# Seven-tap convolution and SwiGLU on one core: how the first pair of blocks is convolved and laid out

## The chip, the core and the metric

One core of a Trainium2 chip. Its engines run their own queues of instructions side by side: TensorE (PE, with a row of its own for weight loads, PEld), VectorE (DVE), ScalarE (ACT), GpSimd (POOL) and SyncE (SP), which issues most transfers (DMA). The metric is the device time of one execution in microseconds. Three timed runs of the kernel before have a median of 776.05 us (775.36 to 777.06).

## What is computed

The input x is 8 sequences of 4096 tokens of 192 channels, float32. Each channel is convolved along its sequence with seven causal taps, which are the softmax of one of eight rows of weights (24 channels a row). The 32768 tokens that result go through a SwiGLU block with 1536 hidden features:

```python
w = exp(weight - max(weight)); w = w / (sum(w) + 1e-9)          # 8 x 7
x = sum over k of w[head of channel, k] * x_padded[token + k]   # padded by 6 zeros in front
g = x @ w_gate; val = x @ w_val
out = (g * sigmoid(g) * val) @ w_out
```

The weights are held as float16, sums are float32.

## The kernel before

**Blocks and chunks.** A block is 512 tokens (TB), a pair is two blocks, so there are 64 blocks in 32 pairs. For each block the hidden features are taken in 12 chunks of 128. `Block.first` makes one chunk's gate and value in two PSUM banks: since 192 = 3 x 64, three steps each, a gate matmul on the upper 64 rows of the array beside a value matmul on the lower 64, 512 tokens long. `Block.gate` lets ScalarE apply SiLU and VectorE multiply by the value; the product h is float16. `Block.piece` multiplies h with w_out, in eight matmuls of 192 columns a chunk, one block behind the gates (`second` hands them out, four units per chunk; the last chunk of a block takes the block's own first four). Every 24 units ScalarE copies the sum out (`evacuate`) and SyncE stores it. Chunks are counted through the whole kernel: block 0 is chunks 0 to 11, block 1 is 12 to 23, block 2 begins at 24.

**Banks.** A gate has two banks (PLAN's gate), a value three (val); in block 0 the chunks in PLAN's `third` put the gate in the bank named `run` instead. So a gate waits for SiLU two or three chunks back, a value for the product three chunks back.

**The first pair.** Blocks 0 and 1 are convolved on TensorE. x is loaded (x_sb), cast to float16 (x16), turned by TensorE (`turn`, `turn_a`) and copied to SBUF with the padding in front (xcA, xcC, xcA1, xcC1). Channels 0 to 127 are A, the last 64 are C, held twice. `conv_a` multiplies shifted views of A with diagonal matrices of the taps, once with their high parts (dg["hi"]) and once with the low rests (dg["lo"]), `conv_c` does C with dg["C"]. The sums are folded: the first 256 tokens of 64 channels lie on partitions 0 to 63, the last 256 on 64 to 127. ScalarE copies them to foldA (two halves of A) and foldC. The gates want 64 channels on both halves of the partitions and 512 tokens in a row. In block 0 `double` does that: matmuls with `twin`, an identity twice over, and copies out (`unfold`, D0, D1, D2). In block 1 `spread_out` does it by transfers from foldA1 and foldC1 to D01b and D2b, four for each.

**Order by hand.** The program is written in the order in which each engine takes it. Block 0's C is convolved after its A has been doubled, and `doubleC` comes between the first gates of chunks 0 and 1. Block 1's A sums are made behind the first gates (`lateA("hi")`) and after chunk 1, `outA` follows at chunk 2, `lateC` at 4 and `outC` at 5.

**Later pairs.** They are loaded as squares of 32 tokens by 32 channels (`emit_load`: sqA in parts 0 and 1, sqB in parts 2 and 3, two transfers each; headA and headB where a sequence starts), turned by VectorE (`emit_turn`) and convolved by three engines in three groups a pair (`Group`; A of the first block, B, A of the second block): ScalarE makes the first product (`start_d`, into the PSUM bank run) and two more, VectorE adds taps to the first, GpSimd makes the rest, adds everything and writes xc (`join`). `swap` has SyncE copy xc with its partition halves exchanged (xs). `plan_group` puts the steps at chunks; PLAN's `opening` holds them for pair 1 as (turn, start, ScalarE's two, VectorE's, GpSimd's, join, swap). Pair 1's squares are issued at the start, as soon as the first two pieces of x have been turned; later ones at the chunks in PLAN's `load`, counted from 24 times the pair.

**Queues.** SyncE issues in program order: x, pair 1's squares, the first of pair 2's, the eight transfers of `spread_out`, further squares, the swaps and the outputs. GpSimd's queue first builds masks and casts x, issues the loads of w_gate and w_val in thirds of four chunks and of w_out, then works on the groups.

Of the kernel before, what the change touches and what calls it, by code (L numbers as in the profile page):

```python
# [17 lines left out]
    opening=(  # L18
# [3 lines left out]
    ),  # L22
    gate=2, val=3, lead=4, third=(5, 8, 11),
# [4 lines left out]
def kernel(  # L28
# [53 lines left out]
    def emit_load(q, part):  # L82
        head = q % ppb == 0
        if part == 2:
            squares[q, "A"] = headA if head else xpool.tile(
                [P, HIST + 2 * TB], fp32, tag="sqA", name="sqA"
            )
            squares[q, "B"] = headB if head else xpool.tile(
                [P, HIST + TB], fp32, tag="sqB", name="sqB"
            )  # L90
        for k in range(2):
# [3 lines left out]
            else:  # L95
# [3 lines left out]
            n = n // SQ + 1 - skip // SQ  # L99
            nc.sync.dma_start(  # L100
                out=tile_[quad * SQ : (quad + 1) * SQ, skip:].rearrange("p (n c) -> p n c", c=SQ),
# [82 lines left out]
    load_w(0, 4, 0)  # L184
    cast_c(nc.gpsimd.tensor_copy, 0, 2)
    cast_c(nc.gpsimd.tensor_copy, 2, 4)
    load_w(0, 4, 1)
# [4 lines left out]
    for b in range(2):  # L192
# [24 lines left out]
        for n, shape, dt in (  # L217
            ("xtA", [P, TB], fp32),
            ("xtC", [P, DB + TB], fp16),
            ("sumA", [P, 2, TB], fp32),  # L220
            ("idle", [P, 2, TB], fp32),
            ("xtA1", [P, DB + TB], fp16),
# [21 lines left out]
    def turn_a(subs):  # L244
        for s in subs:
            ins = nc.tensor.matmul(
                early["xtA"][:, ts(s, P)], x16[:, s, colA], ident, start=True, stop=True
            )
        return ins
# [8 lines left out]
    turned = turn_a((0, 1))  # L258

    if n_pairs > 1:  # L260
        sync_after(nc.sync.nop(), turned, "squares after x")
        for part, _ in PLAN["load"]:
            emit_load(1, part)
    turn_a((2, 3))
    warm(SUBS, SUBS)

    xcA, xcC, xcC1, xcA1 = (
        const_pool.tile([P, pad + TB], fp16, tag=n, name=n) for n in ("xcA", "xcC", "xcC1", "xcA1")
# [21 lines left out]
    diagonal(dg["lo"], lo)  # L290
    two = const_pool.tile([P, 1], fp32, tag="two", name="two")
    nc.scalar.copy(xcA[:, pad:], early["xtA"])
# [25 lines left out]
    def double(out, fold):  # L318
# [3 lines left out]
    foldA, foldA1 = (const_pool.tile([P, 2, TH], fp16, tag=n, name=n) for n in ("foldA", "foldA1"))  # L322
    foldC, foldC1 = (const_pool.tile([P, TH], fp16, tag=n, name=n) for n in ("foldC", "foldC1"))
    D0, D1, D2, D2b = (
        const_pool.tile([P, TB], fp16, tag=n, name=n) for n in ("D0", "D1", "D2", "D2b")
    )
    D01b = const_pool.tile([P, 2, TB], fp16, tag="D01b", name="D01b")

    def unfold(copy, out, pair):
        copy(out[:, :].rearrange("p (h t) -> p h t", h=2), pair[:, :, 0:TH])  # L330

    conv_a(early["sumA"], xcA, dg["hi"], True)
    spread(1)
# [3 lines left out]
    turn(early["xtA1"], colA, SUBS, hist=True)  # L337
    nc.vector.tensor_copy(wn[:, 1, :], tap_rows[1])
    nc.vector.tensor_copy(hi[:, 1, :], wn[:, 1, :])
    nc.vector.tensor_tensor(hi[DB:P, 1, :], wn[DB:P, 1, :], hi[DB:P, 1, :], op=ALU.subtract)  # L340
    diagonal(dg["C"], hi[:, 1, :])
    nc.scalar.copy(foldA, early["sumA"][:, :, 0:TH])
    early["xtC1"] = pool0.tile([P, DB + TB], fp16, tag="xtC", name="xtC")
    turn(early["xtC1"], colC, SUBS, hist=True)
    nc.vector.tensor_copy(xcA1, early["xtA1"][:, DB - pad :])
    pairs = [
        pool0.tile([P, 2, TB], fp32, tag=n, name=n) for n in ("sumA", "idle")
    ]
    double(pairs[0], foldA[:, 0, :])
    double(pairs[1], foldA[:, 1, :])  # L350
    sumC = pool0.tile([P, TB], fp32, tag="taps0", name="taps0")
    conv_c(sumC, xcC)
    unfold(nc.scalar.copy, D0, pairs[0])
    unfold(nc.vector.tensor_copy, D1, pairs[1])
    nc.vector.tensor_copy(xcC1, early["xtC1"][:, DB - pad :])
    nc.scalar.copy(foldC, sumC[:, 0:TH])
# [16 lines left out]
    class Group:  # L373
# [17 lines left out]
        def start_d(self):  # L391
            self.aD = tpool.tile([P, TB], fp32, tag="run", name="run")
# [34 lines left out]
    class Block:  # L427
# [20 lines left out]
        def first(self, j, steps=range(3)):  # L448
# [5 lines left out]
            lo, hi = self.operands()  # L454
            for i in steps:
                (a, ca), (b, cb) = lo[i], hi[i]
                nc.tensor.matmul(g, w[0:DB, ca, f], a[0:DB, :], start=(i == 0), stop=(i == 2))  # L457
                nc.tensor.matmul(v, w[DB:P, cb, f], b[DB:P, :], start=(i == 0), stop=(i == 2))  # L458
# [50 lines left out]

    def doubleC():  # L510
        for (r, _), bank in zip(sides, pairC):
            nc.tensor.matmul(bank[:, 0:TH], twin[r, :], foldC[r, :], start=True, stop=True)
        for (r, t0), bank, copy in zip(sides, pairC, (nc.scalar.copy, nc.vector.tensor_copy)):
            copy(D2[:, t0 : t0 + TH], bank[:, 0:TH])

# [3 lines left out]
    A, B = (D01b[:, 0, :], D01b[:, 1, :]), D2b  # L519
    early_operands = [((d, 0), (e, 1), (f, 2)) for d, e, f in ((D0, D1, D2), (*A, B))]  # L520
    early_operands = [(o, o) for o in early_operands]
# [39 lines left out]
    def late_sums():  # L561
        late["sum"] = apool.tile([P, 2, 512], fp32, tag="acc", name="acc")

    def lateA(part):
        if part == "hi":
            late_sums()
        conv_a(late["sum"], xcA1, dg[part], part == "hi")

    def lateC():
        late_sums()  # L570
        conv_c(late["sum"][:, 0, :], xcC1)

    def spread_out(out, fold):
        for r, _ in sides:
            for half, (f, _) in enumerate(sides):
                nc.sync.dma_start(out=out[r, ..., half * TH : (half + 1) * TH], in_=fold[f])  # L576
# [141 lines left out]
```

## Time and profile before

| | |
|---|---|
| time of the profiled execution | 773.12 us |
| its span | 771.4 us |
| median of the timed runs | 776.05 us |
| granted clock of TensorE | 1.00 |
| weight loads busy (PEld) | 599.6 us, 78% |
| instructions | 27963 |
| first gate matmul | 10.03 us |
| x_sb's four transfers | 3.1 us to landing |
| w_out's transfer | 10.1 us to landing |
| first pair that uses xs | 37.29 us |

The span is the time from the first to the last record of the trace; the rest of the reported time lies around it. In a row of stages the columns are: from and to, length, then busy time (and instructions) of PE, PEld, DVE, ACT and POOL, granted clock, share of the DMA engines' time (above one where packets overlap) and GB/s. A timeline row has its start, its length, engine, line, operation, what it writes and reads, how many were merged, and in brackets the idle time before it and what ended it. A group's row has busy time and mean nanoseconds of one, then the idle time before it. SPq rows are SyncE's issues, not the transfers themselves.

### The profile page before, as it was taken

What the parts mean: (1) busy time and instruction counts of PE and PEld (TensorE: products, weight loads), DVE (VectorE), ACT (ScalarE), POOL (GpSimd) and SP (SyncE); (2) the same over time, 40 slices, a digit from 0 to 9 for tenths busy, and PEclk for the clock granted to TensorE, in tenths of its full rate; (3) what the DMA queues carried; (4) which work ended last, traced back from release to release, by engine and by line L of the source; (5) the groups of instructions that cost most, each with busy time, mean ns of one, the idle gap of its engine ahead of it and who ended that gap; (6) DMA issues with size and microseconds to landing.
All of it is one profiled execution on the core that took longest, in us unless ns stands there. A gap on an engine that the chain in (4) does not pass through costs nothing.

```text
span 771.4 us, 27963 instructions
## 1 busy us (share of the span) xinstructions
PE 764.5 (99%) x10881; PEld 599.6 (78%) x10881; DVE 658.0 (85%) x1042; ACT 662.6 (86%) x1189; POOL 666.9 (86%) x643
## 2 busy tenths in 40 slices
PE   9899999999999999999999999999999999999998
PEld 4577777777878878888887888888888888888886
DVE  6788888888888888888888888898888888888875
ACT  7788888888888888888888888888888888888875
POOL 7798988888988889988889888899888899888850
PEclk9999999999999999999999999999999999999999
DMA  9434344433444434444334444334343434443211
GB/s 179 96 82 88 84 90 86 92 88 78 89 92 90 88 82 89 86 86 100 82 81 83 97 82 94 86 82 87 82 98 83 89 86 86 89 90 87 65 47 53
DMA packets 255670, 67.36 MB, mean 87 GB/s; under 512 B 207920, under 2 KB 255536, under 8 KB 255536
## 3 DMA queue, kind: packets, MB, share of 16 engines
q1 hardware_dynamic: 252720, 63.80, 39.6%
q0 software_dynamic: 2800, 1.77, 1.7%
q8 instruction: 85, 1.39, 0.8%
q14 instruction: 49, 0.40, 0.2%
q10 hardware_dynamic: 16, 0.00, 0.0%
HBM read 29.55 MB, written 25.17 MB: 71 GB/s over the span
## 4 chain that ended last, share of the span: by engine, by line
PE 99%; DMA 0%; SPq 0%; DVE 0%; ACT 0%; issue 0%; DVEq 0%
PE val L458 49%; PE acc L469 34%; PE gate L457 13%; PE idle L229 0%; PE acc L669 0%; DMA D2b<-foldC 0%; PE sumA L304 0%; PE acc L304 0%; SPq L576 0%; PE val L669 0%; PE run L669 0%; PE taps L312 0%; PE acc L312 0%; PE xtC L240 0%; DVE dghi L280 0%; ACT silu L462 0%
## 5 line engine op out<-in xcount | busy, mean ns | idle before, releaser
L464 DVE TENSOR_TENSOR h<-silu,val 128x512 f16<-128x512 f16 x768 | 509.0, 680 | 102.7 <-ACT silu L462 69.9
L462 ACT ACTIVATE silu<-gate 128x512 f16<-128x512 f32 x768 | 453.2, 594 | 79.5 <-PE gate L457 75.0
L469 PE MATMUL acc<-wo_sb,h 64*128 64x192 f16 x6048 | 469.0, 243 | 0.0
L415 POOL TENSOR_TENSOR t<-t,t 128x512 f32<-128x512 f32 x310 | 393.9, 1271 | 65.4 <-ACT t L386 44.8
L469 PEld LDWEIGHTS <-h 64*128 64x128 f16 x6048 | 399.3, 94 | 58.7
L458 PE MATMUL val<-xc,w_sb 64*128 64x512 f16 x1116 | 409.7, 376 | 0.0
L457 PE MATMUL gate<-xc,w_sb 64*128 64x512 f16 x1116 | 409.7, 376 | 0.0
L457 PE MATMUL gate<-xs,w_sb 64*128 64x512 f16 x1116 | 360.0, 376 | 0.0
L458 PE MATMUL val<-xs,w_sb 64*128 64x512 f16 x1116 | 360.0, 376 | 0.0
L458 PEld LDWEIGHTS <-w_sb 64*128 64x128 f16 x2304 | 208.9, 94 | 98.5 <-DMA D01b<-foldA 1.2
L457 PEld LDWEIGHTS <-w_sb 64*128 64x128 f16 x2304 | 208.7, 94 | 4.6 <-issue 1.4
L421 POOL TENSOR_TENSOR xc<-t,aD 128x512 f16<-128x512 f32 x93 | 118.2, 1271 | 7.3
L408 POOL TENSOR_SCALAR t<-xtA,wn 128x512 f32<-128x512 f32 x155 | 106.2, 697 | 2.0 <-DVE xtA L111 2.0
L386 ACT ACTIVATE t<-xtA,wn 128x512 f32<-128x512 f32 x124 | 88.4, 713 | 0.0
L507 ACT COPY o<-acc 128x384 f32<-128x384 f32 x126 | 60.4, 479 | 18.9 <-PE acc L469 8.4
L403 DVE SCALAR_TENSOR_TENSOR aD<-xtA,wn,run 128x512 f32<-128x512 f32 x62 | 46.0, 741 | 0.0
L386 ACT ACTIVATE t<-xtB,wn 128x512 f32<-128x512 f32 x62 | 44.3, 715 | 0.0
L408 POOL TENSOR_SCALAR t<-xtB,wn 128x512 f32<-128x512 f32 x62 | 42.4, 698 | 0.5 <-DVE xtB L111 0.5
L393 ACT ACTIVATE run<-xtA,wn 128x512 f32<-128x512 f32 x62 | 42.5, 686 | 0.2 <-DVE xtA L111 0.2
L111 DVE STREAM_TRANSPOSE xtA<-sqA 128x544 f32<-128x544 f32 (+1 forms) x48 | 34.6, 721 | 0.0
L403 DVE SCALAR_TENSOR_TENSOR run<-xtB,wn,run 128x512 f32<-128x512 f32 x31 | 23.2, 750 | 0.8 <-ACT run L393 0.8
L403 DVE SCALAR_TENSOR_TENSOR run<-xtA,wn,run 128x512 f32<-128x512 f32 x31 | 23.2, 750 | 0.0
(102 smaller groups left out, 172.9 us busy)
## 6 DMA issues: line engine op xcount, KB each, us to landing
out_dram<-o SPq DMA_DIRECT2D x127, 192.0 KB, 2.0
sqA<-in_x_dram SPq DMA_DIRECT2D x96, 132.0 KB, 3.1
xs<-xc SPq DMA_DIRECT2D x186, 64.0 KB, 2.0
sqB<-in_x_dram SPq DMA_DIRECT2D x96, 68.0 KB, 2.4
headA<-in_x_dram SPq DMA_DIRECT2D x28, 128.0 KB, 2.9
headB<-in_x_dram SPq DMA_DIRECT2D x14, 68.0 KB, 2.2
headB<-in_x_dram SPq DMA_DIRECT2D x14, 64.0 KB, 2.5
x_sb<-in_x_dram SPq DMA_DIRECT2D x4, 192.0 KB, 3.1
```

The lines of the kernel that those rows point to most:

```text
L386: mul(parts[-1], *self.tap(k))
L393: nc.scalar.mul(self.aD, *self.tap(0))
L403: nc.vector.scalar_tensor_tensor(out=self.aD, in0=v, scalar=s, in1=run, op0=ALU.mult, op1=ALU.add)
L408: self.product(k, lambda t, v, s: nc.gpsimd.tensor_scalar(t, v, scalar1=s, scalar2=1.0, op0=ALU.mult, op1=ALU.mult), self.parts)
L415: nc.gpsimd.tensor_tensor(self.parts[0], self.parts[0], t, op=ALU.add)
L421: nc.gpsimd.tensor_tensor(xc, self.parts[0], self.aD, op=ALU.add)
L457: nc.tensor.matmul(g, w[0:DB, ca, f], a[0:DB, :], start=(i == 0), stop=(i == 2))
L458: nc.tensor.matmul(v, w[DB:P, cb, f], b[DB:P, :], start=(i == 0), stop=(i == 2))
L462: nc.scalar.activation(s, self.g.pop(j), AF.Silu)
L464: nc.vector.tensor_tensor(h, s, self.v.pop(j), op=ALU.mult)
L469: ins = nc.tensor.matmul(acc, self.h[j][r, ts(s, P)], wo_r[r, j, :], start=first and j == 0, stop=not first and j == NCH - 1, skip_group_c ...
L507: nc.scalar.copy(self.o[:, 2 * half : 2 * half + 2, :], self.acc[:, :, 0:D])
```

## The change

Block 0's C is convolved, folded and doubled before its first gate, and `doubleC` goes. Block 1's sums of A come after chunks 1 and 3. Block 1's C is no longer convolved on TensorE: xcC1 is made in folded form, each half of the partitions with its own 256 tokens and the six before, VectorE makes taps 0 and 1, GpSimd the other five, and GpSimd's last add writes foldC1. Block 1's gates read the folded tiles themselves: each chunk in two rounds of 256 tokens, one from foldA1 and foldC1, the other from swapA1 and swapC1, whose halves are exchanged by two transfers for A and two for C. Pair 1's sqA comes in two parts, the second behind these transfers; pair 2's squares are not issued before chunk 6. Group B of pair 1 holds its running sum in SBUF (runB). Block 0's third gate bank is used from chunk 2. The first half of x is turned into two tiles; the taps of C are spread before the first sum; both loads of the first third of weights are issued before GpSimd's casts.

```diff
-        (9, 11, (12, 13), (12, 13), 12, 13, 18),
-        (None, -1, (2, 4), (-1, 2), 2, 4, 11),
-        (14, 16, (18, 20), (17,), 20, 21, 31),
+        (9, 12, (13, 14), (13, 14), 12, 14, 20),
+        (None, 1, (2, 5), (2, 4), 2, 5, 14),
+        (18, 20, (22, 23), (21,), 20, 23, 31),
     ),
-    gate=2, val=3, lead=4, third=(5, 8, 11),
+    gate=2, val=3, lead=4, third=(2, 5, 8, 11),
...
-    def emit_load(q, part):
+    def emit_load(q, part, half=None):
...
+            if half is not None:
+                first = TB // SQ + 1
+                skip, row, n = ((skip, row, first), (first * SQ, row + first * SQ, n - first))[half]
...
     load_w(0, 4, 0)
+    load_w(0, 4, 1)
...
-    turned = turn_a((0, 1))
+    turned = turn_a(0)
...
-            emit_load(1, part)
-    turn_a((2, 3))
-    warm(SUBS, SUBS)
+            emit_load(1, part, None if part > 1 else 0)
+    turn_a(2)
+    spread(1)
+    warm(SUBS)
...
     conv_a(early["sumA"], xcA, dg["hi"], True)
-    spread(1)
     turn(early["xtC"], colC, 0)
     nc.scalar.copy(xcC[:, pad:], early["xtC"][:, 0:TB])
     conv_a(early["sumA"], xcA, dg["lo"], False)
...
     nc.scalar.copy(foldA, early["sumA"][:, :, 0:TH])
+    sumC = pool0.tile([P, TB], fp32, tag="taps0", name="taps0")
+    conv_c(sumC, xcC)
+    nc.scalar.copy(foldC, sumC[:, 0:TH])
+    pairs = [pair("sumA"), pair("idle")]
     double(pairs[0], foldA[:, 0, :])
     double(pairs[1], foldA[:, 1, :])
     unfold(nc.scalar.copy, D0, pairs[0])
     unfold(nc.vector.tensor_copy, D1, pairs[1])
+    xtA1 = pool0.tile([P, DB + TB], fp16, tag="xtC", name="xtC")
+    turn(xtA1, colA, SUBS, hist=True)
+    nc.vector.tensor_copy(xcA1, xtA1[:, DB - pad :])
+    xtC1 = pool0.tile([P, DB + TB], fp16, tag="taps0", name="taps0")
+    turn(xtC1, colC, SUBS, hist=True)
+    pairs.append(pair("idle"))
+    double(pairs[2], foldC)
+    unfold(nc.scalar.copy, D2, pairs[2])
+    xcC1 = const_pool.tile([P, pad + TH], fp16, tag="xcC1", name="xcC1")
+    for r, t0 in sides:
+        nc.vector.tensor_copy(xcC1[r, :], xtC1[r, DB - pad + t0 :][:, 0 : pad + TH])
...
         def start_d(self):
-            self.aD = tpool.tile([P, TB], fp32, tag="run", name="run")
+            if (self.p, self.g) == (1, 1):
+                self.aD = const_pool.tile([P, TB], fp32, tag="runB", name="runB")
+            else:
+                self.aD = tpool.tile([P, TB], fp32, tag="run", name="run")
...
+            passes = [(g, v, *self.operands())]
+            if self.n == 1:
+                halves = [slice(0, TH), slice(TH, TB)]
+                passes = [
+                    (g[:, a], v[:, b], [(x[k], c) for *x, c in early_operands[1]],
+                     [(x[k], c) for *x, c in early_operands[1]])
+                    for k, (a, b) in enumerate((halves, halves[::-1]))
+                ]
+            for g, v, lo, hi in passes:
+                for i in steps:
+                    (a, ca), (b, cb) = lo[i], hi[i]
+                    nc.tensor.matmul(g, w[0:DB, ca, f], a[0:DB, :], start=(i == 0), stop=(i == 2))
+                    nc.tensor.matmul(v, w[DB:P, cb, f], b[DB:P, :], start=(i == 0), stop=(i == 2))
...
+    def tapC1(k):
+        return xcC1[:, k : k + TH], wn[:, 1, k : k + 1]
+    v, s = tapC1(0)
+    nc.vector.tensor_scalar(sumC1, v, scalar1=s, scalar2=None, op0=ALU.mult)
+    v, s = tapC1(1)
+    nc.vector.scalar_tensor_tensor(
+        out=sumC1, in0=v, scalar=s, in1=sumC1, op0=ALU.mult, op1=ALU.add
+    )
+    for k in range(2, K):
+        v, s = tapC1(k)
+        t = oneC1 if k > 2 else poolC1
+        nc.gpsimd.tensor_scalar(t, v, scalar1=s, scalar2=1.0, op0=ALU.mult, op1=ALU.mult)
+        if k > 2:
+            nc.gpsimd.tensor_tensor(poolC1, poolC1, oneC1, op=ALU.add)
+    nc.gpsimd.tensor_tensor(foldC1, poolC1, sumC1, op=ALU.add)
+    early_operands = [
+        (((D0, 0), (D1, 1), (D2, 2)),) * 2,
+        ((foldA1[:, 0, :], swapA1[:, 0, :], 0), (foldA1[:, 1, :], swapA1[:, 1, :], 1),
+         (foldC1, swapC1, 2)),
+    ]
...
-    def spread_out(out, fold):
-        for r, _ in sides:
-            for half, (f, _) in enumerate(sides):
-                nc.sync.dma_start(out=out[r, ..., half * TH : (half + 1) * TH], in_=fold[f])
+    def exchange(out, fold):
+        for r, q in ((0, 1), (1, 0)):
+            nc.sync.dma_start(out=out[sides[r][0]], in_=fold[sides[q][0]])
...
     def outA():
         nc.scalar.copy(foldA1, late["sum"][:, :, 0:TH])
-        spread_out(D01b, foldA1)
+        exchange(swapA1, foldA1)
     def outC():
-        nc.scalar.copy(foldC1, late["sum"][:, 0, 0:TH])
-        spread_out(D2b, foldC1)
+        exchange(swapC1, foldC1)
+        if n_pairs > 1:
+            for part in (0, 1):
+                emit_load(1, part, 1)
...
-    at_chunk(1, lambda: lateA("lo"))
-    at_chunk(2, outA)
-    at_chunk(4, lateC)
-    at_chunk(5, outC)
+    at_chunk(1, lambda: lateA("hi"))
+    at_chunk(3, lambda: lateA("lo"))
+    at_chunk(3, outA)
+    at_chunk(4, outC)
...
-            at_chunk(base + c, lambda q=q, part=part: emit_load(q, part))
+            at_chunk(max(base + c, 6), lambda q=q, part=part: emit_load(q, part))
...
                     block.first(0, (0, 1))
-                    doubleC()
                     block.first(1, (0, 1))
-                    lateA("hi")
```

86 lines of the change are left out of this document (29 added, 57 removed).

## The prediction

> **What bounds the kernel now.** I read the page's engine table first, then the busy time by stages, then the chain of waits, TensorE's and SyncE's timelines and the groups by form.
>
> ```profile
> PE 764.5 (99%) x10881; PEld 599.6 (78%) x10881; DVE 658.0 (85%) x1042; ACT 662.6 (86%) x1189; POOL 666.9 (86%) x643
> 22.00:24.00 2.00, 0.80 (x6) 0.22 (x4) 1.48 (x3) 0.92 (x2) 1.51 (x3) 1.00 0.42 82
> 24.00:28.00 4.00, 2.70 (x34) 1.69 (x33) 1.53 (x3) 2.04 (x4) 2.38 (x2) 1.00 0.48 92
> 28.00:32.00 4.00, 4.00 (x61) 2.93 (x59) 3.63 (x6) 3.47 (x7) 3.40 (x4) 1.00 0.58 115
> ```
>
> TensorE is busy 99% of the span; from 28 us to the tail every stage is full at a granted clock of 1.00. The one hole is 22 to 26 us. So a change is worth what it moves the moment from which TensorE is full, and nothing in the later stages can be won by it. TensorE's timeline and the chain say what the hole is:
>
> ```profile
> 22.36 0.39 PE L457 MATMUL gate<-D01b,w_sb 64*128 64x512 f16 x1 [0.25 <-DMA D01b<-foldA]
> 23.70 0.37 PE L458 MATMUL val<-D01b,w_sb 64*128 64x512 f16 x1 [0.95 <-DMA D01b<-foldA]
> 24.68 0.39 PE L457 MATMUL gate<-D2b,w_sb 64*128 64x512 f16 x1 [0.38 <-DMA D2b<-foldC]
> 25.98 0.39 PE L458 MATMUL val<-D2b,w_sb 64*128 64x512 f16 x1 [0.91 <-DMA D2b<-foldC]
> ...
> 24.04 1.89 DMA D2b<-foldC
> ```
>
> Block 1's first chunk waits for its unfolded operands, four times. Its six matmuls (three pairs, .215 us from pair to pair) should end .65 after they begin; the first began 22.36, the last ends its issue at 26.20. SyncE's timeline tells why the operands are late:
>
> ```profile
> 6.75 8.24 SPq L100 DMA_DIRECT2D sqA<-in_x_dram  x4
> 15.03 3.75 SPq L100 DMA_DIRECT2D sqB<-in_x_dram  x2
> 18.90 3.17 SPq L576 DMA_DIRECT2D D01b<-foldA  x4
> 22.17 2.46 SPq L576 DMA_DIRECT2D D2b<-foldC  x4
> ```
>
> foldA's copy on ScalarE (L579) ends at 15.46, but SyncE is still issuing squares until 18.8, then issues eight transfers one after another.
>
> **The change, part by part.** Every time is on the scale of this execution (span 771.4, reported time 773.12; the three timed runs have a median of 776.05, 2.93 more, which I add at the end).
>
> *Until the first gate.* Between 5.47 and 10.03 TensorE does: sumA 0.96, own taps 0.31, xtC 0.33, sumA 0.89, two transposes of block 1 at 0.46 each, two doublings 0.33 and taps 0.89. Afterwards the own taps stand before this (beside one warm-up, so nothing to gain at the start) and a third doubling, 0.22, comes in. First gate 10.0: no gain. The turn of two 128-row pieces into two tiles is worth at most 0.1, which I leave out.
>
> *Block 0.* All six pairs of its first two chunks can now run when D2's copy is done: doubling ends 10.05, copy 0.59 (L330 on ScalarE), so chunks 0 and 1 end at 11.5 (before, with one sum between, 12.55). Left until block 1: sumA twice 0.89, ten chunks at 0.645, first eight acc 0.33: 8.56, which gives 20.1. The third sum (L312, 0.89) is gone. But VectorE must follow: the product of a chunk waits for SiLU and frees the bank that the chunk three later needs. From the first product at 12.2, ten products at 0.62 from start to start and two tap steps at 0.65 (the timeline's spacing) end at 19.7 where SiLU is never late. Laying the instructions of TensorE, ScalarE and VectorE down in their queues' order with these spacings, TensorE waits 1.0 in all for products, in chunks 7, 8 and 11 (bounds nothing and 2.0; the first would give block 1 one microsecond more). Block 1 begins at 21.4, its first chunk ends at 22.05 (26.20 before). The copy of the second doubled tile and the tail are unchanged.
>
> *Operands of block 1.* Foldings stand as they are for one half of the tokens; the other half comes by two transfers instead of four (each L576 issue 0.5 to 0.8). SyncE has half the sqA packets ahead: 8.24 x 17/33 = 4.2, so it is free at 11, and pair 2's sqB no longer stands there. swapA is issued when foldA1 is copied, 15.7 at the latest, and lands (1.9 to 2.1) by 18.4. Queued behind swapC on SyncE: four half sqA, pair 2's sqB; first needed at chunk 18, some 27. wo_sb landed at 19.7 under twice the sqA packets and is wanted at 21.0. So the hole closes with 2 us to spare.
>
> *Twelve matmuls a chunk in block 1.* Pairs of 64x256 instead of 64x512. Not in the trace as such. The chain has these:
>
> ```profile
> 8.88 0.22 PE sumA L320 x2
> 9.10 0.11 PE idle L320 x2
> 9.21 0.89 PE taps L312 x14
> ```
>
> L320 is the same form (64 rows, 128 columns of weights, 256 streamed), second pair 0.11; L469, 192 streamed, goes at 0.08 a pair with a 94 ns weight load under it; L312, 7 pairs of another form, 0.127. Bounds for block 1: 12 x (6 x 0.107 - 0.645), nothing, and 12 x (6 x 0.127 - 0.645) = 1.4. I take L320: 12 x 0.015 = 0.2. The Trainium skill's TensorEngine Tiling, Feature Incompatibilities, says that column tiling switches off fast weight loading; L312 is column-tiled and the new passes are not, which would leave L312's price out, and nothing run so far tests it.
>
> By TensorE alone block 2 then begins at 21.4 + 0.98 + 10.75 (26.32 to 37.07 before, eleven chunks) + 0.2 = 33.3, against 37.07: 3.75 earlier.
>
> *GpSimd's new work.* Ten instructions of 256 elements, in front of all of pair 1's groups. GpSimd is free at 10.63 (end of wo_sb's issue). Their forms are not in the trace:
>
> ```profile
> L415 POOL TENSOR_TENSOR t<-t,t 128x512 f32<-128x512 f32 x310 | 393.9, 1271 | 65.4 <-ACT t L386 44.8 <-DVE h L464 0.7
> L408 POOL TENSOR_SCALAR t<-xtB,wn 128x512 f32<-128x512 f32 x62 | 42.4, 698 | 0.5 <-DVE xtB L111 0.5
> L179 POOL CAST x<-x_sb 128x256 f16<-128x256 f32 x2 | 0.8, 428 | 0.0
> L179 POOL CAST x<-x_sb 128x512 f16<-128x512 f32 x1 | 0.6, 619 | 0.0
> L165 POOL TENSOR_TENSOR twin<-ident 128x128 f16<-128x128 f32 x1 | 0.5, 513 | 0.1
> ```
>
> An add costs at least half of 1.271, 0.64, at most all of it; a line through 128 elements (0.513) and 512 gives 0.77; I take 0.70. A tap product lies between 0.35 and 0.70; the casts lose 30% when halved, so 0.45. Five of each 5.75, eight dependent gaps of 0.07 0.55: 6.3, bounds 5.3 and 10.4. foldC1 at 17.0, swapC lands by 19.8: in time. Then group B and group A, 2 x 0.69 + 4 x 1.33 = 6.7 each (34.60 to 39.92 is four such adds): A's join ends at 30.4. Neither waits for ScalarE's taps, which are earlier than this.
>
> *A shared way into memory.* In the change VectorE reads two operands from SBUF in three steps (sumC1's second and both of group B's, whose run was in PSUM and is now runB) and copies SBUF to SBUF in a fourth, all while GpSimd is busy. Two of VectorE's copies of as many elements, and what GpSimd did beside the second:
>
> ```profile
> 2.45 0.21 DVE L201 CAST ident<-ident 128x128 f16<-128x128 f32 x1
> 2.92 0.84 POOL L140 DMA_DIRECT2D w_sb<-in_moe_w_gate_dram  x1
> 3.42 0.57 DVE L206 COPY own<-mask 8x128 f32<-8x128 f32 x1
> ```
>
> L206 lasts until 0.23 after GpSimd's issue ends, as if it had waited. Against this, GpSimd's cast at 5.97 began under dglo's last 0.13 and took 616, the next one 619. So the cost to GpSimd lies between nothing and their length, 0.3 + 0.45 + 2 x 0.74 = 2.2; I take half, 1.1. The Trainium skill, SBUF — State Buffer, Who interferes with whom, says that a VectorE instruction with two SBUF inputs and a GpSimd one that reads SBUF exclude each other for a whole instruction; L206 agrees with it, and it would have the second rival below.
>
> *Sum.* A's join 31.5; SyncE issues two swaps (0.5 and 0.6), the last at 32.1; landing 2.0 (xs on the page) to 2.9 (this swap before, behind an output): 34.1 to 35.0, I take 34.3, as the queue is quiet there. Block 2's second pair needs it at 33.5 by TensorE and had it at 37.29. So a wait of 0.8 takes the place of one of 3.8, and the gain is 37.29 - 34.3 = 3.0. Pair 1's third group (three products, five adds: 8.7, and 3.5 to land) is there at 43.7, wanted at 46; after that GpSimd, busy 90.7 of 100 us in the later stages, gains on TensorE. 773.12 - 3.0 = 770.1; by the median 773.05.
>
> **The rivals.**
> 1. *GpSimd is in time:* adds at 0.64, no exclusion. Join 29.5, landing 32.2; TensorE's own path decides, 3.75 earlier: 772.3. If the 256-wide pairs cost 0.127 it is 2.5: 773.5. For it: GpSimd's durations vary by under 2% in the whole trace. Against: the 128-element add at 0.513.
> 2. *The exclusion costs its whole length:* join 32.6, last issue 33.2, landing 2.9: 36.1, gain 1.2: 774.85. For it: L206; against: the cast at 5.97.
> 3. *The exchange is late all the same:* transfers at 16 us still queue as sqA's did (8.7 to landing, DMA share 1.95 at 16 to 18). swapA lands at 25.0 instead of the last wait at 25.98, gain 1.0 to 1.5: 774.7. Then the change would not do what it says. Against: half the packets.
> 4. *Slower, by GpSimd:* its 256-wide instructions cost what 512-wide do. foldC1 lies 4.1 later, A's join at 35.6, swap landed 36.2 + 2.9 = 39.1 against 37.29: 1.8 slower, 777.9. It decides from where the ten instructions with their exclusions last over 10.4 (34.5 for the join). Against: the casts fall from 0.619 to 0.428 with the size.
>
> **How the numbers follow.** Forecast 0.42, rivals 0.2, 0.2, 0.1, 0.08. The forecast's own terms (1.1 either way from the exclusion, landing 0.8) give 772.2 to 774.5. The range takes in the first rival's 772.3 and the second's and third's 774.85 with half a microsecond for the spread of the runs: 772.0 to 775.3. A measurement of this kernel tells 0.2%, 1.55 us, from no change: forecast, first rival and a little of the others are faster by more, 0.70; most of rivals 2 and 3 lie within, 0.20; slower 0.10.
>
> **What would show it.** Block 1's first chunk ends near 22 with no wait for a DMA; block 1's pairs are 0.11 apart; foldC1 ends at 17 to 18; block 2's second pair waits for xs, under a microsecond, and everything later is full. Wrong it would be with a DMA wait in block 1, a product chain that holds TensorE more than 1.0 in block 0, GpSimd instructions of 256 near 0.7 and 1.27, or a second hole at block 3.

## The result and the profile after

| | before | after |
|---|---|---|
| median of the timed runs | 776.05 us (775.1 to 777.06, 5 runs) | 771.81 us (771.5 to 773.23, 5 runs) |
| time of the profiled execution | 773.12 us | 773.23 us |
| its span | 771.4 us | 771.5 us |
| first gate matmul | 10.03 us | 12.17 us |
| block 1's first gate | 22.36 us | 24.02 us |
| block 2's first gate | 37.07 us | 36.61 us |
| weight loads busy (PEld) | 599.6 us | 511.1 us |

The ratio of after to before is 0.995, with a 95% interval of 0.9936 to 0.9965: 4.2 us faster by the medians. The two profiled executions differ by 0.11 us, that is by nothing. Both statements are right, and most of this study is about how they fit together.

The stages of the changed kernel, by the table of windows (window, length, busy time and instructions of TensorE, weight loads, VectorE, ScalarE, GpSimd, then granted clock, DMA share, GB/s):

```profile
22.00:24.00 2.00, 2.00 (x25) 1.17 (x21) 1.87 (x4) 1.78 (x4) 1.92 (x2) 1.00 0.46 73
24.00:28.00 4.00, 3.60 (x74) 3.28 (x70) 3.59 (x7) 3.49 (x7) 3.84 (x5) 1.00 0.58 91
28.00:32.00 4.00, 4.00 (x86) 3.72 (x82) 3.26 (x6) 3.10 (x6) 3.76 (x4) 1.00 0.80 153
```

The hole from 22 to 26 us is gone: of the 6 us from 22 to 28 TensorE is busy for 5.60, against 3.50 before. TensorE's timeline shows block 1's first chunk without a wait for a transfer, and its pairs 0.11 us apart (columns: start, length, engine, line, operation; in brackets the idle time ahead and what ended it):

```profile
24.02 0.27 PE L483 MATMUL gate<-foldA,w_sb 64*128 64x256 f16 x1
...
24.13 0.27 PE L483 MATMUL gate<-foldA,w_sb 64*128 64x256 f16 x1
...
24.24 0.27 PE L483 MATMUL gate<-foldC,w_sb 64*128 64x256 f16 x1
...
24.35 0.27 PE L483 MATMUL gate<-swapA,w_sb 64*128 64x256 f16 x1
...
24.57 0.27 PE L483 MATMUL gate<-swapC,w_sb 64*128 64x256 f16 x1
...
27.41 0.51 PE L495 MATMUL acc<-wo_sb,h 64*128 64x192 f16 x8 [0.40 <-SPq L377]
```

The chain of waits of the same execution (start, length, what) shows where the two microseconds were lost again:

```profile
6.02 1.64 PE sumA L313 x20
8.20 1.64 PE sumA L313 x27
9.83 1.12 PE taps L321 x14
...
19.30 0.73 POOL foldC L559
20.06 0.46 SPq L612
...
26.43 0.78 SPq L103
27.41 0.51 PE acc L495 x8
```

The two sums of the opening take 1.64 us each. In the chain of before they took 0.96 and 0.89:

```profile
5.47 0.96 PE sumA L304 x28
...
7.07 0.89 PE sumA L304 x28
```

So in the changed kernel's execution TensorE runs at little more than half its speed until about 10 us; this is called half speed below, and an opening at full speed a quick one. The windows print a granted clock of 1.00 here too, but only because the trace's record of the clock begins later: at 10.28 us in this trace, at 3.79 in that of before. The slowness is read from the matmuls' lengths. And at 27.41 TensorE waits for something that no line of the diff names: L377 is a nop in SyncE's queue (`mark`), behind which the first sum of block 0's outputs stands. SyncE comes to it when swapC has waited for GpSimd's foldC (20.03) and eight issues of squares are done (27.2). TensorE waits for a mark once more, behind pair 2's swaps, which SyncE issues when GpSimd's join has ended (56.25):

```profile
57.57 0.51 PE L495 MATMUL acc<-wo_sb,h 64*128 64x192 f16 x8 [0.30 <-SPq L377]
```

### The profile page after: what moved, and what is told of

It reads as the page before. It is cut to its first block, busy times and chain, and to the rows that moved or that the text cites. A ratio compares the mean times of both kernels' runs of the same rounds, so it can differ in the third digit from the quotient of the medians.

```text
span 771.5 us, 28091 instructions
## 1 busy us (share of the span) xinstructions
PE 766.0 (99%) x10938; PEld 511.1 (66%) x10938; DVE 659.4 (85%) x1044; ACT 658.4 (85%) x1189; POOL 672.8 (87%) x653
## 4 chain that ended last, share of the span: by engine, by line
PE 96%; POOL 2%; SPq 1%; DVE 0%; issue 0%; ACT 0%; POOLq 0%; DVEq 0%
PE gate L483 59%; PE acc L495 32%; PE val L484 4%; SPq L103 1%; POOL t L432 1%; PE idle L232 0%; PE sumA L313 0%; POOL poolC L558 0%; POOL xc L438 0%; POOL oneC L556 0%; PE acc L699 0%; POOL t L425 0%; PE taps L321 0%; SPq L612 0%; PE val L699 0%
## 5 line engine op out<-in xcount | busy, mean ns | idle before, releaser
L495 PEld LDWEIGHTS <-h 64*128 64x128 f16 x6048 | 280.9, 94 | 136.2 <-SPq L377 1.5
L495 PE MATMUL acc<-wo_sb,h 64*128 64x192 f16 x6048 | 359.1, 243 | 0.7 <-SPq L377 0.7
```

The lines of the kernel that those rows point to most:

```text
L495: ins = nc.tensor.matmul(acc, self.h[j][r, ts(s, P)], wo_r[r, j, :], start=first and j == 0, stop=not first and j == NCH - 1, skip_group_c ...
```

## Experiments

All of the kernels compute the whole result. "Before" beside a ratio is the kernel before on the same chip, measured in the same session. There were three sessions after the first, one for experiments 1, 2 (its first kernel) and 3, one for 4 to 6 and the rest of 2, one for 7 and 8; the medians of before lie between 775.8 and 776.2 in all four, so a few tenths between kernels of different sessions mean little. Besides their time, runs give the mean clock that TensorE was granted; this turned out to matter.

**1. The kernel before, again, and its squares alone moved.** No edit in the first.

> The kernel before, unchanged, for its clock: in the first profile of before the opening's matmuls ran at full speed from 4.6 us, in that of after only from 10.4. Theory: the moment differs from run to run and is mostly late, so that the profile of before was one of the quick ones. Then this one has a median of 776.0, and if its own profile is near 776 its first gate starts at about 12 us and its sums take 1.6 us instead of 0.9; if near 773, at 10 us. Rival, that the change itself makes the opening slow: the first gate starts at 10 us with a time of 776 as well.

776.55 us (773.43 to 777.07, 12 runs), ratio 1.0004 [0.9992, 1.0016]. Its profiled execution is one whose opening runs at half speed, as in the changed kernel, so the change isn't what makes openings slow. And yet it takes 773.43, where the expectation had a time near 776 for such an opening:

```profile
6.16 1.71 PE L304 MATMUL sumA<-xcA,dghi 64*64 64x256 f16 x28
8.85 1.60 PE L304 MATMUL sumA<-xcA,dglo 64*64 64x256 f16 x28
...
12.51 0.39 PE L457 MATMUL gate<-D,w_sb 64*128 64x512 f16 x1
```

The first gate is 2.5 us later than in the first profile, and the end only 0.3: the hole swallows the rest. That is the first thing to learn here. Such an opening costs the kernel before little, because block 1 waits for its transfers anyway, and it costs the changed kernel 1.7 (experiment 5).

The other one takes from the change only the order of the squares:

```diff
-            emit_load(1, part)
+            emit_load(1, part, None if part > 1 else 0)
...
         spread_out(D2b, foldC1)
+        if n_pairs > 1:
+            for part in (0, 1):
+                emit_load(1, part, 1)
...
-            at_chunk(base + c, lambda q=q, part=part: emit_load(q, part))
+            at_chunk(max(base + c, 6), lambda q=q, part=part: emit_load(q, part))
```

> Before, with the squares alone moved: the second half of pair 1's sqA behind the transfers to D2b, pair 2's squares not before chunk 6. Theory that SyncE's squares made block 1's operands late: D01b's four transfers are issued as soon as foldA is copied, D2b's follow, the last lands some 2.5 us earlier than before, 773.4 to 774. Rival, that the exchanged halves and the early convolution make the gain: 775 or more.

773.23 us (772.91 to 774.95, 11 runs), ratio 0.9975 [0.9964, 0.9985], a little less than expected. D2b's waits fall to 0.2 in all. In TensorE's waits (engine, line, releaser: total, times, longest) the mark now stands in their place:

```profile
PE acc L472 <- SPq L366: 2.2, 1, 2.2
```

Order alone closes the wait for transfers, and the squares behind it hold SyncE's marks.

**2. The change without its order, and without its exchange.** First the changed kernel with the squares in the order of before:

```diff
-            emit_load(1, part, None if part > 1 else 0)
+            emit_load(1, part)
...
-            at_chunk(max(base + c, 6), lambda q=q, part=part: emit_load(q, part))
+            at_chunk(base + c, lambda q=q, part=part: emit_load(q, part))
```

> After, with pair 1's sqA whole at the start and pair 2's squares from chunk 1, as before. Theory: swapA is issued 2 to 4 us later, behind the squares, swapC follows it, and a wait for DMA comes back in block 1's first chunk, about 1 us: 772.5 to 773.5. Rival 1, that the order of the squares does not matter since four transfers instead of eight are enough: 771.8. Rival 2, that the second halves and pair 2's squares, which after issues just behind swapC, hold TensorE through SyncE's marks: faster than after, 771 or less.

773.72 us (772.25 to 774.97, 12 runs), ratio 0.9972 [0.9962, 0.9982]; profiled at 772.25 with a quick opening. swapC comes 0.4 late where 1 was expected, and a wait for a transfer is back, as the theory had it:

```profile
PE val L484 <- DMA swapC<-foldC: 0.4, 1, 0.4
```

Then the changed kernel with four transfers each to D01b and D2b and 512-wide matmuls in block 1:

```diff
-        for r, q in ((0, 1), (1, 0)):
-            nc.sync.dma_start(out=out[sides[r][0]], in_=fold[sides[q][0]])
+        for r, _ in sides:
+            for half, (f, _) in enumerate(sides):
+                nc.sync.dma_start(out=out[r, ..., half * TH : (half + 1) * TH], in_=fold[f])
```

> The change, with block 1's operands laid out by four transfers each for A and C, as before, and 512-wide matmuls, so only the exchange is undone; the squares stay later. Theory (the order of SyncE's queue closed the hole, not the smaller exchange): SyncE issues D01b's last transfer near 19.6 and D2b's near 22.6, landing at 21.6 and 24.6; block 1's C operands come 0 to 0.7 late and the marks 2.2 later than in the changed kernel, which gives +0.3 to +1.5. Rival (the exchange is what matters): D01b and D2b late by 2 to 3, as before, and the time 774 or more.

774.71 us (773.35 to 775.33, 12 runs), ratio 0.9984 [0.9972, 0.9997]. Its waits:

```profile
PE acc L490 <- SPq L379: 1.4, 2, 1.0
PE val L479 <- DVE h L485: 0.8, 1, 0.8
PE val L479 <- DMA D2b<-foldC: 0.6, 1, 0.6
```

The change run beside it has a median of 773.35 (experiment 4), 1.4 less. With openings at half speed alike it is profiled at 775.27 against 773.12 to 773.23 of the change, 2.1 more: 0.6 stands in the wait for D2b and 0.7, against the first profile of the change, in longer waits for marks (SyncE issues four transfers more ahead of them); the rest isn't traced to a line. So the exchange is worth 1.4 to 2.1. The waits are those of the theory (D2b 0 to 0.7 late, not 2 to 3), the time is that of its rival (774 or more). The order is worth 0.4 to 1.0 in the changed kernel (772.25 against the 771.2 to 771.8 of its quick runs, experiment 4). Either part nearly closes the hole without the other; that only the order matters was wrong.

**3. Block 1's C back on TensorE** (chunk 4, copied to foldC1 by ScalarE, `outC` at 5; VectorE's and GpSimd's taps of it go, everything else as changed):

```diff
...
+    def lateC():
+        late["sum"] = apool.tile([P, 2, 512], fp32, tag="acc", name="acc")
+        conv_c(late["sum"][:, 0, :], xcC1)
...
+        nc.scalar.copy(foldC1, late["sum"][:, 0, 0:TH])
         exchange(swapC1, foldC1)
...
-    at_chunk(4, outC)
+    at_chunk(4, lateC)
+    at_chunk(5, outC)
```

> After, with block 1's C convolved by TensorE at chunk 4 as before (0.89 us more for TensorE), nothing on GpSimd and VectorE for it, exchange by two transfers kept. Theory that GpSimd's chain is what ends late: groups of pair 1 are done 6 us earlier, SyncE is not held by foldC, and the time is 771.0 to 772.0. Rival, that the move off TensorE is worth its 0.89: 772.7 or more.

772.08 us (770.83 to 772.55, 5 runs), ratio 0.9954 [0.9938, 0.997], 0.1 above what was expected; profiled at 770.84. TensorE's one wait between 9 and 100 us is 0.3 for a product, and block 2's second value pair begins at 34.80. GpSimd ends A's join at 29.99 in place of 32 to 33.9. The 14 matmuls of C that the change takes from TensorE last 0.89; in their place GpSimd works 7.1 us ahead of pair 1's groups, and xs can then come too late for block 2. That part of the change brings no time, it costs some 0.6 (against the 771.43 of experiment 5, quick like this one).

**4. The changed kernel again.**

> The changed kernel once more. Theory: between its executions one thing differs, the moment from which TensorE runs at full speed. Where that is near 4.5 us (14 matmuls of a first sum in 0.96 to 1.0), the first gate comes near 10.0 and the time is 771.3 to 771.7; where it is near 10 us (the sum takes 1.64, first gate near 12.2), the time is 772.6 to 773.3. So the timed runs stand in two groups some 1.2 us apart, and the median is 771.5 to 772.7. Rival: the 771.5 and the 773.2 seen before are ordinary scatter: then the profile's time doesn't go with the length of its first sums.

773.35 us (771.22 to 773.89, 7 runs), ratio 0.9959 [0.9942, 0.9975]. With the five of the result, the twelve runs of the changed kernel lie in two groups, 771.2 to 771.8 (five) and 772.7 to 773.9 (seven), and their median is 772.9; the 773.35 here is above the expected 772.7, as more of these runs are of the later sort. Both its profiles (773.12, 773.23) have openings at half speed. There is no profile of this very kernel with a quick opening, so that the quicker group is the one with quick openings is inferred; the next experiment has one, of a kernel that differs only later. In this second profile the mark isn't waited for, and instead:

```profile
35.77 0.38 PE L483 MATMUL gate<-xs,w_sb 64*128 64x512 f16 x1
37.49 0.37 PE L484 MATMUL val<-xs,w_sb 64*128 64x512 f16 x1 [1.34 <-DMA xs<-xc]
```

This is the wait that the prediction had (0.8, for the swap of GpSimd's last group), 0.5 larger. The value matmul begins at 37.49, as it did before, in an execution of the same 773.12:

```profile
37.50 0.38 PE L458 MATMUL val<-xs,w_sb 64*128 64x512 f16 x1
```

**5. Pair 2's squares later still**, behind the marks:

```diff
-            at_chunk(max(base + c, 6), lambda q=q, part=part: emit_load(q, part))
+            if q == 2:
+                c = {2: 16, 3: 18, 0: 20, 1: 22}[part] - base
+            at_chunk(base + c, lambda q=q, part=part: emit_load(q, part))
```

> The change, with pair 2's squares issued at chunks 16, 18, 20 and 22 instead of all behind the exchange at chunk 6. Theory: SyncE's marks, which TensorE's first acc of chunk 12 or 13 waits for, stand behind those eight issues (the queue is held until 27.2 us); with the issues later the wait of 0.7 to 2 us at 27.4 is gone, and the time falls by 0.5 to 1.5 against the changed kernel of the same call, at the same length of the first sums. Rival: the wait on the mark only takes a pause that TensorE would have had anyway (pair 1's swap of group A, GpSimd's join 33.9): block 2's second pair then waits for xs or its product, as long, and the time is the same within 0.3.

772.64 us (771.3 to 773.85, 6 runs), ratio 0.9954 [0.9937, 0.9972]; profiled at 771.43. No wait for a mark on TensorE's matmuls is left. The quick runs, 771.3 and 771.4, are no lower than those of the change (771.2 and 771.4 on the same chip): there the rival holds, and the mark took a pause that xs would have taken. The other four have a median of 772.9 against 773.4 of the change's five, with ranges that overlap; whether the mark costs some 0.5 there stays open. The profiled execution has the quick opening, and shows the change as the prediction had meant it:

```profile
5.46 0.98 PE L313 MATMUL sumA<-xcA,dghi 64*64 64x256 f16 x28
...
6.70 0.96 PE L313 MATMUL sumA<-xcA,dglo 64*64 64x256 f16 x28
...
34.08 0.38 PE L483 MATMUL gate<-xc,w_sb 64*128 64x512 f16 x1
...
35.80 0.37 PE L484 MATMUL val<-xs,w_sb 64*128 64x512 f16 x1 [1.13 <-DMA xs<-xc]
```

The value matmul comes at 35.80, 1.70 before that of the kernel before (37.50), and the time is 1.69 less (773.12 to 771.43).

**6. Group B's run back in PSUM.** VectorE's two steps read one operand from SBUF, as before, and chunk 2's gate has no third bank.

```diff
-    gate=2, val=3, lead=4, third=(2, 5, 8, 11),
+    gate=2, val=3, lead=4, third=(5, 8, 11),
...
-            if (self.p, self.g) == (1, 1):
-                self.aD = const_pool.tile([P, TB], fp32, tag="runB", name="runB")
-            else:
-                self.aD = tpool.tile([P, TB], fp32, tag="run", name="run")
+            self.aD = tpool.tile([P, TB], fp32, tag="run", name="run")
```

> The change, with group B's running sum back in the PSUM bank run, which is then no longer lent to chunk 2's gate. VectorE's two tap steps on it read one operand from SBUF instead of two. Theory (each engine is prolonged by the other while VectorE reads two operands from SBUF): those two steps fall from 1.10 and 1.12 to 0.75, GpSimd's products beside them from 0.53 and 0.80 to 0.48, its ten instructions from 7.1 to 6.5, and A's join ends 0.3 to 0.6 earlier; the time changes by under 0.4, as the missing third bank costs TensorE some of it at chunk 3 and 4. Rival: the steps last long because their output goes to SBUF, or by the size of what GpSimd does beside them: then GpSimd's instructions stay as they are.

773.57 us (771.68 to 775.25, 12 runs), ratio 0.9974 [0.9961, 0.9987]. The first theory holds, and its rival falls: the second step still writes to SBUF (aD) and is as short as the first. VectorE's and GpSimd's timelines of the changed kernel (its first profile):

```profile
16.96 1.12 DVE L420 SCALAR_TENSOR_TENSOR runB<-xtB,wn,runB 128x512 f32<-128x512 f32 x1
...
19.47 1.10 DVE L420 SCALAR_TENSOR_TENSOR aD<-xtB,wn,runB 128x512 f32<-128x512 f32 x1
```

```profile
12.95 0.47 POOL L556 TENSOR_SCALAR poolC<-xcC,wn 128x256 f32<-128x256 f16 x1 [1.24 <-DVE xcC L370]
...
16.80 0.73 POOL L558 TENSOR_TENSOR poolC<-poolC,oneC 128x256 f32<-128x256 f32 x1
17.62 0.80 POOL L556 TENSOR_SCALAR oneC<-xcC,wn 128x256 f32<-128x256 f16 x1
18.50 0.72 POOL L558 TENSOR_TENSOR poolC<-poolC,oneC 128x256 f32<-128x256 f32 x1
19.30 0.73 POOL L559 TENSOR_TENSOR foldC<-poolC,sumC 128x256 f16<-128x256 f32 x1
20.01 1.79 POOL L425 TENSOR_SCALAR t<-xtB,wn 128x512 f32<-128x512 f32 x2
```

and of this kernel:

```profile
16.16 0.75 DVE L418 SCALAR_TENSOR_TENSOR run<-xtB,wn,run 128x512 f32<-128x512 f32 x1
...
18.68 0.74 DVE L418 SCALAR_TENSOR_TENSOR aD<-xtB,wn,run 128x512 f32<-128x512 f32 x1
```

```profile
16.82 0.48 POOL L554 TENSOR_SCALAR oneC<-xcC,wn 128x256 f32<-128x256 f16 x1
...
18.88 1.36 POOL L423 TENSOR_SCALAR t<-xtB,wn 128x512 f32<-128x512 f32 x2
```

Each of the two meetings costs VectorE 0.36 and GpSimd 0.32 or 0.43: together with 0.06 at one product beside sumC1, which this kernel keeps, 0.8 of GpSimd's time in the change. The lines also show how. The add that GpSimd has begun keeps its 0.73; VectorE's step ends 0.55 after that add; and GpSimd's product ends 0.34 after VectorE's step. They take turns, and each pays what is left of the other's instruction. The Trainium skill, SBUF — State Buffer, Who interferes with whom, says that a VectorE instruction with two inputs in SBUF contends with a GpSimd instruction that reads SBUF; the trace agrees. GpSimd's A join ends 0.8 earlier after its start than in the change (20.2 against 21.0 us). The time isn't lower, since the missing third bank opens a hole in TensorE at chunk 4:

```profile
19.47 0.37 PE L481 MATMUL gate<-D,w_sb 64*128 64x512 f16 x1 [2.06 <-DVE aD L418]
```

Five of its twelve runs are slower than 774.8, by 1.7 from median to median of the two sorts. The change has none there, and this led to the next experiment.

**7. The hole filled, nothing else.** The granted clocks of the runs (the first five of before have none on record), with the least busy time of TensorE that a profile of the kernel shows in a window of 3.4 us, laid every 1.7 us between 10 and 60 us:

```
kernel                          least busy   runs at 0.999-1.000   at 0.997-0.998   at 0.996
before                          1.38         11 (773.2 to 775.6)   26 (774.9-776.3) 45 (775.7-778.3)
squares later (1)               1.24          6 (772.9 to 773.2)    5 (774.1-775.0)  0
run in PSUM (6)                 1.34          7 (771.7 to 773.6)    5 (774.9-775.3)  0
the change (two sessions)       2.06         12 (771.2 to 773.9)    0                0
change, squares as before (2)   2.61         12 (772.3 to 775.0)    0                0
change, four transfers (2)      2.34         12 (773.4 to 775.3)    0                0
squares later still (5)         2.27          6 (771.3 to 773.9)    0                0
C on TensorE (3, two sessions)  3.05         11 (770.6 to 772.6)    0                0
```

In the three kernels with a stretch of 1.24 to 1.38 us busy a part of the runs loses clock, in the five others, with 2.06 or more, none does. The loss is 0.002 or 0.004 of 771 us, 1.5 or 3.1 us; the runs of before are longer by about that, 1.6 and 2.8 from median to median. A stretch of 3.4 us at half speed loses 1.7, so one or two such stretches would do it. The Trainium skill, TensorE: Matmul & The Clock Gate, What's actually happening, says that the clock is halved after an idle window of some 3.4 us and whole again after a busy one; the sizes agree, though TensorE was never idle for so long here.

The traces' own record of the clock says more than the windows print. In all 13 profiles the stretch at full clock begins between 3.8 and 10.3 us and lasts a whole number, 223 to 225, of 3.413 us. At the tail it ends after such a stretch with TensorE busy for 1.12 us or less, and goes on after one with 1.46 (experiment 2, first kernel). So the clock is granted in stretches of 3.413 us, whose boundaries fall differently in each execution, and at the tail it is lost after one busy for less than some 1.12 to 1.46 us, which is near the 1.24 to 1.38 above. In the first profile of before boundaries at 20.9, 24.3 and 27.7 split the hole, with TensorE busy for 2.21 and 2.12, and this execution kept its clock; the worst position would have left 1.15. This is not the whole account: 71 of 82 runs of before lost clock, more than the positions in that profile would give, and its second profile, with the late opening, has no window under 2.48.

To see whether the hole does it, seven idle matmuls were put into the kernel before, where block 1's first chunk waits:

```diff
+                if self.n == 1 and j == 0 and i == 2:
+                    fill(self.v[1], 1)
                 nc.tensor.matmul(g, w[0:DB, ca, f], a[0:DB, :], start=(i == 0), stop=(i == 2))
+                if self.n == 1 and j == 0 and i != 1:
+                    fill(self.v[1], 3)
                 nc.tensor.matmul(v, w[DB:P, cb, f], b[DB:P, :], start=(i == 0), stop=(i == 2))
...
+    def fill(bank, n):
+        for _ in range(n):
+            nc.tensor.matmul(bank, twin, D0, start=True, stop=True)
```

> The kernel before, with seven idle matmuls (128 rows, 512 columns, into the bank of the next chunk's value) put where block 1's first chunk waits for its operands; nothing waits less. Theory (TensorE's clock goes back to half speed for one or two of its 3.4 us windows after the hole, in most timed runs of before: their granted clock averages 0.996 or 0.998, that is 6.8 or 3.4 us at half speed, and they take 776 to 777.5 and 775 to 776, against 773.2 to 774.5 of those at 1.0): with the hole filled TensorE has no window under half busy, the runs at 0.996 and 0.998 are gone, and the median falls from 776.1 to 773.2 to 774.5. Rival (the 3 us between profiled and timed executions come from elsewhere, as memory or the ends of the program): the median stays at 776 or rises by the matmuls' length, up to 1.5.

774.06 us (773.6 to 777.49, 12 runs), ratio 0.9981 [0.9969, 0.9993]. The windows of before, and of this kernel (busy time of TensorE, then clock, DMA share, GB/s):

```profile
20.40:23.80 3.40, 2.20 (x24) 1.00 0.45 84
22.10:25.50 3.40, 1.38 (x6) 1.00 0.38 75
23.80:27.20 3.40, 2.10 (x23) 1.00 0.43 77
```

```profile
20.40:23.80 3.40, 3.35 (x31) 1.00 0.41 76
22.10:25.50 3.40, 2.99 (x22) 1.00 0.41 81
23.80:27.20 3.40, 2.87 (x19) 1.00 0.33 62
```

Nine of twelve runs are at 1.000 (773.6 to 774.6), against two of seventeen of before beside them, and the median falls from 775.78 to 774.06, by matmuls that compute nothing. That three runs still lost clock, in a kernel whose profile has no such window under 2.87, isn't explained, and the theory hadn't expected it.

**8. A denser opening.** In the kernel of experiment 3, run again beside it:

```diff
     turn_a(2)
+    warm(SUBS)
     spread(1)
-    warm(SUBS)
+    warm(SUBS, SUBS)
```

> The changed kernel with block 1's C on TensorE again, the same as before in this study, as the one to compare with in this call: 770.8 to 770.9 where TensorE's full speed begins near 4.5 us, 772.0 to 772.6 where it begins later; no run at 0.998 or below, since no window of its profile has TensorE under 3.0 of 3.4 us busy; median 770.9 to 772.3.

> The same kernel with two more idle matmuls of 512 columns in the opening, one ahead of the second spreading of the taps and one behind it. Theory (a window of 3.4 us opens the clock only if TensorE is busy in some 80% of it, and the few small matmuls from 3.8 to 5.4 us leave too little in a window that ends between 5 and 7 us): full speed now begins by 7 us at the latest in nearly all executions, they lie together at 770.8 to 771.4, and the median falls by 0.3 to 1.2 where the other's runs are mostly of the late sort. Rival (the moment is set by something else, or the two matmuls cost their 0.43 to 0.86 on the path to the first gate): the two groups stay, each 0.2 to 0.9 later.

771.59 us (770.62 to 772.63, 6 runs), ratio 0.9943 [0.9926, 0.996], and 771.81 (770.66 to 773.0, 6 runs), ratio 0.9948 [0.9929, 0.9967]. The theory falls, and no run supports its 80%: in each three runs are quick (770.6 to 770.8) and three are not, and those are 0.3 later with the added matmuls. What decides the moment of full speed in the opening stays open.

The kernel of experiment 3 is the best found: group by group 0.7 and 0.9 below the change (eleven runs, 770.6 to 770.8 and 772.1 to 772.6, against 771.2 to 771.8 and 772.7 to 773.9). The two weren't measured in one session.

## Why the prediction came out as it did

The forecast was 773.05 and the measured median 771.81, within its range. The mechanism of the gain is confirmed: the hole closes, and xs takes its place as the wait. But two terms of the sum were wrong, in opposite directions. The gain in an execution that keeps its clock was forecast at 3.0 and is 1.7 or less; the 2.93 added for the timed runs isn't there in the changed kernel. That the two nearly cancel is luck. So is some of the 771.81: three of its five runs are quick, and the median of all twelve is 772.9.

- *The hole closes, the exchange lands in time:* right. No transfer is waited for in block 1, and order and exchange each do a part (1, 2). This is against the third rival, an exchange late all the same.
- *Pairs of 64x256 at 0.11:* right; block 1 lasts from 22.10 to 34.08 in experiment 5, 11.98, where the terms give 11.93.
- *First gate at 10.0:* 10.24 with a quick opening, where C's matmuls, moved forward, wait 0.41 for their taps (dgC), and 11.9 to 12.2 with one at half speed. This is the step that failed first. The profile of before had a quick opening, and one profile can't tell that it is one of two. In before one at half speed costs 0.3, in the change 1.7.
- *Block 0:* TensorE waits 0.8 for products, forecast 1.0; block 1 begins 11.9 after the first gate, forecast 11.4. The terms written down, 20.1 and 1.0, give 21.1 and not the 21.4 that the sum goes on with.
- *GpSimd:* products at 0.47 and adds at 0.73 (taken 0.45 and 0.70), 0.8 by exclusion (taken 1.1, bounds 0 to 2.2): well sized. L206, from which the exclusion was argued, has a single input and ran beside a DMA issue; the test that it wasn't is experiment 6. The lower bound of the ten instructions, 5.3, is 5.5 by its own terms, which changes nothing. GpSimd's ten start at 11.0 or 12.6 to 13.0 instead of 10.63, as they wait for VectorE's second copy of xcC1, which the sum had left out. A's join ends at 32.0 (forecast 31.5), or at 33.6 to 33.9.
- *The swap:* the last landing was taken at 2.2 after SyncE's last issue began, with 2.9 as its bound; it took 3.2 in experiment 5 (from 32.54 on), 3.3 in the second profile of the change and 2.0 in the first. This is the largest part of what the forecast missed with a quick opening: landing in 2.0, xs would have been there at 34.5 (an estimate), near the forecast's 34.3. So the wait for xs is 1.1 to 1.3, forecast 0.8, and the gain on the profiled scale 1.7 with the quick opening and none with the other, forecast 3.0. It is nearer to the second rival's 1.2, but by the late start and the landing, not by its exclusion.
- *"By the median 773.05", that is 2.93 added for the timed runs:* wrong in kind. This was no constant of the measurement; most of it is clock that most runs of before lose, and with the hole closed the twelve runs of the change lose none. Filling the hole (7) shows that the hole is a cause.

So the gain is two gains. The medians of the runs that kept their clock are 773.9 (11 runs of before) and 772.9 (12 of the change), 1.0 apart. All runs of before have a median of 776.1, so of 3.2 us in all some 2.2 is clock; experiment 7 shows 1.7 of it by itself. The remaining 1.0 of the 4.2 is the luck of five runs. Of the rivals, the first (GpSimd in time) is what experiment 3 has made of the kernel by taking C off GpSimd; the second falls with the 0.8 measured for the exclusion, the fourth with the 0.47 and 0.73 of the instructions.

SyncE's marks were unforeseen. The prediction named what is queued behind swapC, the squares, and asked only when those are needed, not what else stands in that queue; TensorE itself stood there. In the change it costs nothing that can be measured with a quick opening, since xs comes as late; otherwise perhaps 0.5 (5). With the squares alone moved (1) and with four transfers (2) it is the longest wait.

Open stay: what sets the moment of full speed in the opening, why all 13 profiled executions kept their clock when most timed ones of before did not (none of them has a stretch under 2.05 us busy ahead of the tail, by where its boundaries fall), why the swap's landing varies, and the three filled runs that lost clock.

## What to carry to other kernels

Before a wait is priced, ask whether it leaves TensorE some 40% busy or less over 3.4 us (the kernels above with 61% or more lost nothing): then it may cost the clock for the next stretches too, 1.6 or 2.8 us beside a hole of 2.5 here, and even idle matmuls in it paid. Compare profiles only after checking that their openings run at the same speed, by the length of like matmuls; a wait that disappears also stops hiding what lies ahead of it. And list everything in a queue behind a moved transfer, the nops that only carry order included.

## What the runs showed of the hardware

- TensorE's full speed begins at different moments in executions of one kernel: in before at 3.79 and 10.20 us by the clock record of its two traces, and the 28 matmuls of the first sum take 0.96 and 1.71 us. The profile's windows print 1.00 for both.
- The clock is granted in stretches of 3.413 us: in all 13 traces the full clock lasts 223 to 225 of them. At the tail it ends after one that is 1.12 us busy or less, and not after one with 1.46.
- Losses of clock come in steps: the runs of before are at 1.000, 0.998 and 0.996, and 773.2 to 775.6, 774.9 to 776.3 and 775.7 to 778.3 us.
- A VectorE step with two operands in SBUF takes 1.10 to 1.12 beside GpSimd, and 0.75 with one of them in PSUM; GpSimd's 256-element product beside it takes 0.80 instead of 0.48.
- The swap's transfer takes 2.0 us in the median of the changed kernel; for pair 1's first group A its second half took 2.0 in the first profile, 3.3 in the second and 3.2 in experiment 5. Why was not tried.
